# Attention plus GELU MLP on one core: a rewritten front, a moved GEMM fill, and q,k transposes in the score banks

## The chip, the cores and the metric

One core of one Trainium2 chip. The metric is the device time of one execution in microseconds; lower is better. Executions of one kernel on one chip are compared with executions of the kernel before on the same chip. Each ratio below is the mean time of one kernel's fast runs over that of the other's of the same rounds, so not quite the ratio of the medians quoted.

## The reference

Causal attention with a forgetting gate for 8 batches, 8 heads, 576 positions, head size 64, then an MLP with exact GELU over 4608 tokens, 512 to 2048 to 512.

```python
scores = scale * q @ k.T                       # per batch and head
decay  = cum[:, None] - cum[None, :]           # cum = cumsum(log(clip(f)))
attn   = softmax(where(causal, -1e9, scores + decay))
x      = (attn @ v) as [B*S, H*D]
out    = gelu(x @ w_in) @ w_out
```

The decay is folded into v: `wT` holds exp of minus the cumulated log gate, v is multiplied by it, and a 65th column of the AV product gives the softmax's sum.

## The kernel before

For each batch: load q and k (cast to bf16) and v; transpose q and k of four head pairs on TensorE, copy them from PSUM with VectorE; per pair four score tiles, one exp each on ScalarE, causal masks on GpSimd; AV; normalize; transpose into `xT_sb`; then the first GEMM (`gemm1`, 16 blocks of four matmuls, a GELU each). The second GEMM of the batch before (`gemm2`, 64 matmuls) is fed in small pieces ("fill") between the attention steps of the next batch, so that TensorE does not idle behind the exps.

```python
s_psum = tile_pool(name="s_psum", bufs=2, space=PSUM)   # score tiles [P, 2, 512] fp32
o_psum = tile_pool(name="o_psum", bufs=2, space=PSUM)   # AV outputs, transposes
...
    def transposes(b, i, which):
        src = qk_of[b][which]
        ps = o_psum.tile([P, 2, JT // 2, PT], BF16, tag="o", name="ps_t")
        ...                                             # 6 transposes, then 4 copies
    for b in range(B):
        fill = gemm2(b - 1) if b else iter(())
        load_qk(b + 2)
        load_v(b + 2)
        for i in range(HP):
            for t in range(4):
                scores(b, i, t)
                ...                                     # AV of pair i - 1
                take(fill, 2)
        ...
        for ffb in range(n_ff):
            gemm1(b, ffb)
            if b + 1 < B:
                if ffb % 2 == 1:
                    transposes(b + 1, ffb // 4, (ffb // 2) % 2)
```

Each set of transposes, q's or k's, is a tile of its own, and q's and k's of a pair are two gemm1 blocks apart.

The softmax here doesn't subtract the row's maximum and nothing guards it: scores larger than these inputs give would overflow.

Of the kernel before, what the change touches and what calls it, by code (L numbers as in the profile page):

```python
# [8 lines left out]
FP32 = mybir.dt.float32  # L9
# [5 lines left out]
P = 128  # L15
S = 576
# [33 lines left out]
def kernel(  # L50
# [22 lines left out]
    ctx.enter_context(tc.manual_schedule())  # L73

    consts = ctx.enter_context(tc.tile_pool(name="consts", bufs=1))
    qk_pool = ctx.enter_context(tc.tile_pool(name="qk", bufs=2))
    v_pool = ctx.enter_context(tc.tile_pool(name="v", bufs=2))
    e_pool = ctx.enter_context(tc.tile_pool(name="e", bufs=2))
    x_pool = ctx.enter_context(tc.tile_pool(name="x", bufs=3))
    g_pool = ctx.enter_context(tc.tile_pool(name="g", bufs=2))  # L80
    o_pool = ctx.enter_context(tc.tile_pool(name="outs", bufs=4))
# [4 lines left out]

    qk_of, v_of = {}, {}

    def load_qk(b, h0=0, h1=H):
        if b >= B:  # L90
            return
        if b not in qk_of:
            qk_of[b] = (
                qk_pool.tile([PT, H, JT * D], BF16, tag="q", name=f"q{b}"),
                qk_pool.tile([PT, H, JT * D], BF16, tag="k", name=f"k{b}"),
            )
        for src, dst in zip((q, k), qk_of[b]):
            nc.gpsimd.dma_start(  # L98
                dst[:, h0:h1, :],
                src[b, h0:h1].rearrange("h (p j) d -> p h (j d)", j=JT),  # L100
            )

    def load_v(b, h0=0, h1=H):
        if b >= B:
            return
        if b not in v_of:
            v_of[b] = v_pool.tile([P, H, NBLK, D], FP32, tag="v", name=f"v{b}")
        vt = v_of[b]
        for h in range(h0, h1):
            nc.sync.dma_start(  # L110
                vt[:, h, 0:4, :],
                v[b, h, 0:512].rearrange("(n p) d -> p n d", p=P),
            )
        nc.sync.dma_start(
            vt[:, h0:h1, 4, :], v[b, h0:h1, 448:S].rearrange("h p d -> p h d")
        )

    f_sb = consts.tile([BH, S], FP32)
    nc.sync.dma_start(f_sb, f.rearrange("b h s -> (b h) s"))
    for i in range(HP):  # L120
        load_qk(0, 2 * i, 2 * i + 2)
    load_v(0)


    ident_bf = consts.tile([P, P], BF16)
    make_identity(nc, ident_bf)
    ident_fp = consts.tile([P, P], FP32)
    make_identity(nc, ident_fp)
    qA = [consts.tile([P, S], BF16, name=f"qA{i}") for i in range(HP)]
    qB = [consts.tile([P, S], BF16, name=f"qB{i}") for i in range(HP)]  # L130
    kT = [consts.tile([P, S], BF16, name=f"kT{i}") for i in range(HP)]
# [5 lines left out]
    w_out_sb = consts.tile([P, n_ff, d_model], BF16)  # L137
    w_in_r = moe_w_in.rearrange("(ko ki) f -> ki ko f", ki=P)
    w_out_r = moe_w_out.rearrange("(ko ki) dm -> ki ko dm", ki=P)
    for kt in range(n_dm):  # L140
        nc.gpsimd.dma_start(w_in_sb[:, kt, :], w_in_r[:, kt, :])
    load_qk(1)
    load_v(1)
    for kt in range(0, n_ff, 4):
        nc.gpsimd.dma_start(w_out_sb[:, kt : kt + 4, :], w_out_r[:, kt : kt + 4, :])


    wT = consts.tile([P, NBLK, BH], FP32)
# [7 lines left out]
    nc.scalar.activation(lf, f_sb, Act.Ln)  # L156
    nc.vector.tensor_tensor_scan(cum, ones, lf, 0.0, Alu.mult, Alu.add)
    nc.scalar.activation(wk, cum, Act.Exp, bias=cum[:, S // 2 : S // 2 + 1], scale=-1.0)
    psw = o_psum.tile([P, NBLK, BH], FP32, tag="o", name="psw")

    xT_sb = consts.tile([P, n_dm, N_tok], BF16)


    def transposes(b, i, which):

        src = qk_of[b][which]
        ps = o_psum.tile([P, 2, JT // 2, PT], BF16, tag="o", name="ps_t")
        for h in range(2):
            for j in range(JT // 2):
                nc.tensor.transpose(  # L170
                    ps[:, h, j, :],
                    src[:, 2 * i + h, 2 * j * D : 2 * (j + 1) * D],
                    ident_bf[:PT, :PT],
                )
        for h in range(2):
            dst = (qA[i], qB[i])[h] if which == 0 else kT[i]
            rows = dst[h * D : (h + 1) * D, :].rearrange(
                "d (p j two) -> d two p j", j=JT // 2, two=2
            )
            for odd in range(2):  # L180
                nc.vector.tensor_copy(  # L181
                    rows[:, odd],
                    ps[odd * D : (odd + 1) * D, h].rearrange("d j p -> d p j"),
                )

    vw_of = {}

    def weigh_v(b, i):

        if b not in vw_of:  # L190
            vw_of[b] = v_pool.tile([P, H, NBLK, D + 1], BF16, tag="vw", name=f"vw{b}")
        hs = slice(2 * i, 2 * i + 2)
        bh = b * H + 2 * i
        w = wT[:, :, bh : bh + 2].rearrange("p n h -> p h n")
        nc.gpsimd.tensor_tensor(  # L195
            vw_of[b][:, hs, :, 0:D],
            v_of[b][:, hs, :, :],
            w.unsqueeze(3).to_broadcast([P, 2, NBLK, D]),
            Alu.mult,
        )  # L200
        nc.gpsimd.tensor_copy(vw_of[b][:, hs, :, D], w)

    e_of = {}

# [29 lines left out]
    def attend(b, i, h, ms):  # L234
        if (b, i, h) not in o_of:
            o_of[b, i, h] = o_psum.tile([P, NBLK, D + 1], FP32, tag="o", name="o")
        o = o_of[b, i, h]
        for m in ms:
            for n in range(m + 1):
                t, c = where(n, m)  # L240
                nc.tensor.matmul(  # L241
                    o[:, m, :],
                    e_of[b, i, t][:, h, c : c + P],
                    vw_of[b][:, 2 * i + h, n, :],
                    start=(n == 0),
                    stop=(n == m),
                )

    def normalize(b, i, h):
        if (b, i) not in x_of:  # L250
            x_of[b, i] = x_pool.tile([P, NBLK, 2, D], BF16, tag="x", name="x")
        o = o_of[b, i, h]
        r = x_pool.tile([P, NBLK], FP32, tag="r", name="r")
        nc.vector.reciprocal(r, o[:, :, D])  # L254
        nc.vector.tensor_tensor(  # L255
            x_of[b, i][:, :, h, :],
            o[:, :, 0:D],
            r.unsqueeze(2).to_broadcast([P, NBLK, D]),
            Alu.mult,
        )  # L260
# [30 lines left out]
    def gemm2(c):  # L291

        t0 = c * TC
        for ts in range(n_sub):
            ps = m_psum.tile([P, d_model], FP32, tag="m", name="ps2")
            for kt in range(n_ff):
                nc.tensor.matmul(  # L297
                    ps,
                    g_of[c][kt][:, ts * P : (ts + 1) * P],
                    w_out_sb[:, kt, :],  # L300
                    start=(kt == 0),
                    stop=(kt == n_ff - 1),
                )
                if kt == n_ff - 1:
                    ot = o_pool.tile([P, d_model], FP32, tag="ot", name="ot")
                    nc.vector.tensor_copy(ot, ps)  # L306
                    nc.sync.dma_start(
                        out[t0 + ts * P : t0 + (ts + 1) * P, :], ot
                    )
                yield  # L310
# [4 lines left out]
                return  # L315


    for i in range(HP):
        transposes(0, i, 0)
        transposes(0, i, 1)  # L320
    for n in range(NBLK):
        nc.tensor.transpose(psw[:, n, :], wk[:, K0[n] : K0[n] + P], ident_fp[:BH, :BH])
    nc.vector.tensor_copy(wT[:, 0:4, :], psw[:, 0:4, :])
    nc.vector.tensor_copy(wT[D:P, 4, :], psw[D:P, 4, :])
    for i in range(HP):
        weigh_v(0, i)

    for b in range(B):
        fill = gemm2(b - 1) if b else iter(())
        load_qk(b + 2)  # L330
        load_v(b + 2)
        for i in range(HP):
            for t in range(4):
                scores(b, i, t)
                if i:
                    if t == 0:
                        attend(b, i - 1, 0, (4, 3))
                    elif t == 1:
                        attend(b, i - 1, 0, (2, 1, 0))
                        normalize(b, i - 1, 0)  # L340
                    elif t == 2:
                        attend(b, i - 1, 1, (4, 3))
                    else:
                        attend(b, i - 1, 1, (2, 1, 0))
                        normalize(b, i - 1, 1)
                if i >= 2 and t == 1:
                    to_xT(b, i - 2)
                take(fill, 2)
        i = HP - 1
        take(fill, 4)  # L350
        attend(b, i, 0, (4, 3, 2, 1, 0))
        normalize(b, i, 0)
        to_xT(b, i - 1)
        take(fill, 4)
        attend(b, i, 1, (4, 3, 2, 1, 0))
        normalize(b, i, 1)
        take(fill, 8)
        to_xT(b, i)
        take(fill, 999)
        for ffb in range(n_ff):  # L360
            gemm1(b, ffb)
            if b + 1 < B:
                if ffb % 2 == 1:
                    transposes(b + 1, ffb // 4, (ffb // 2) % 2)
                if ffb % 4 == 2:
                    weigh_v(b + 1, ffb // 4)
    take(gemm2(B - 1), 999)
    for c in range(B, n_chunks):
        for ffb in range(n_ff):
# [32 lines left out]
```

## Time and profile before

| | before |
|---|---|
| time, median (4 runs) | 420.5 us (419.2 to 421.5) |
| first gemm1 matmul of batch 0 | 57.84 us |
| first gemm1 matmul of batch 1 | 102.93 us |
| mean period of the batches after it (gemm1 start to gemm1 start) | 42.78 us |
| TensorE busy | 368.4 of 419.1 us |
| ScalarE: table load at 205.06; exps of 1024 and of 384 columns behind it | 1.28; 1.02 and 0.485 us |
| granted clock from 57.84 to 61.46, first eight gemm1 matmuls of batch 0 | 0.50 |

The starts are read from TensorE's timeline. They cut the run into a front, one batch that has to recover from it, six equal batches, and 59 us of closing GEMMs. The lines behind this reading stand in the prediction.

### The profile page before, as it was taken

Reading aid. Unit: us, or ns where it says so; the run is one execution under the profiler, and the core shown is the slowest. Engines: PE = TensorE matmul, PEld = TensorE weight load, DVE = VectorE, ACT = ScalarE, POOL = GpSimd, SP = SyncE. Lnnn points to the kernel's source line nnn. Section 1 sums busy time; section 2 is a strip of 40 time slices with the busy share of each in tenths; the row PEclk is TensorE's granted clock in tenths of the full one; section 3 lists DMA queues with packets and bytes.
Section 4 is the critical chain, followed back from the end, with each engine's and each line's share of the span. In section 5 each row is a group of like instructions: output and inputs, shape, how many; then the busy total and the mean of one; then the engine's idle time right before and its main releaser. Section 6 shows DMA issues by size and latency. Waiting matters only on the chain.

```text
span 419.1 us, 7515 instructions
## 1 busy us (share of the span) xinstructions
PE 368.4 (88%) x3045; PEld 207.5 (50%) x3045; DVE 207.2 (49%) x466; ACT 215.0 (51%) x291; POOL 129.5 (31%) x262
## 2 busy tenths in 40 slices
PE   1340879899989998999899989998999999999996
PEld 1220645465546554655465546654664456444442
DVE  6930339534954486448634773468355924102001
ACT  3040736872677267725773577447743675350620
POOL 8408460446034603460247024700470042000000
PEclk9999969999999999999999999999999999999999
DMA  9999985801671166216521643100001000102002
GB/s 156 209 193 196 193 186 125 114 28 54 148 109 31 51 152 93 48 51 152 82 58 52 152 65 74 46 31 2 27 27 51 2 25 28 50 0 77 25 25 77
DMA packets 62738, 34.19 MB, mean 82 GB/s; under 512 B 43184, under 2 KB 57520, under 8 KB 62704
## 3 DMA queue, kind: packets, MB, share of 16 engines
q0 software_dynamic: 15328, 13.63, 20.9%
q1 hardware_dynamic: 47376, 20.08, 18.7%
q8 instruction: 24, 0.39, 0.4%
q14 instruction: 10, 0.08, 0.1%
HBM read 37.90 MB, written 9.44 MB: 113 GB/s over the span
## 4 chain that ended last, share of the span: by engine, by line
PE 77%; ACT 8%; POOL 5%; issue 4%; DVE 4%; ACTq 0%; POOLq 0%
PE ps L277 30%; PE ps L297 26%; PE s L210 7%; PE o L241 7%; ACT e L220 6%; PE ps_t L170 4%; POOL e L222 3%; PE ps_x L265 2%; DVE kT L181 2%; ACT L220 1%; DVE qB L181 1%; DVE qA L181 1%; POOL vw L195 1%; POOL q L98 1%; POOL k L98 1%
## 5 line engine op out<-in xcount | busy, mean ns | idle before, releaser
L289 ACT ACTIVATE g<-ps 128x512 bf16<-128x512 f32 x144 | 86.0, 597 | 125.7 <-PE ps L277 125.7
L297 PE MATMUL ps<-w_out_sb,g 128*128 128x512 bf16 x576 | 146.2, 379 | 0.0
L277 PE MATMUL ps<-xT_sb,w_in_sb 128*128 128x512 bf16 x576 | 136.5, 383 | 0.0
L220 ACT ACTIVATE e<-s 128x1024 bf16<-128x1024 f32 (+2 forms) x128 | 105.7, 862 | 56.2 <-PE s L210 47.6
L222 POOL TENSOR_SCALAR_AFFINE_SELECT e<-e 128x256 bf16<-128x256 bf16 x160 | 62.5, 406 | 114.7 <-ACT e L220 114.3
L277 PEld LDWEIGHTS <-w_in_sb 128*128 128x128 bf16 x576 | 54.0, 99 | 58.2 <-issue 3.5
L241 PE MATMUL o<-vw,e 128*128 128x65 bf16 x960 | 53.9, 196 | 17.7 <-POOL e L222 9.7
L297 PEld LDWEIGHTS <-g 128*128 128x128 bf16 x576 | 49.4, 98 | 37.8
L254 DVE RECIPROCAL r<-o 128x5 f32<-128x5 f32 x64 | 12.5, 195 | 110.5 <-PE o L241 110.5
L210 PE MATMUL s<-qA,kT 128*128 128x384 bf16 (+2 forms) x192 | 54.6, 289 | 11.3 <-ACT e L220 10.3
L181 DVE COPY kT<-ps_t 64x288 bf16<-64x288 bf16 x128 | 61.3, 479 | 2.5 <-PE ps_t L170 0.3
L306 DVE COPY ot<-ps 128x512 f32<-128x512 f32 x36 | 24.7, 687 | 75.7 <-PE ps L297 75.7
L210 PEld LDWEIGHTS <-kT 128*128 128x128 bf16 x384 | 37.2, 100 | 47.1 <-issue 17.2
L241 PEld LDWEIGHTS <-e 128*128 128x128 bf16 x960 | 45.5, 99 | 29.7 <-POOL e L222 11.3
L210 PE MATMUL s<-qB,kT 128*128 128x384 bf16 (+2 forms) x192 | 49.7, 290 | 0.0
L195 POOL TENSOR_TENSOR vw<-v,wT 128x640 bf16<-128x640 f32 x32 | 40.8, 1276 | 15.9 <-issue 13.1
L181 DVE COPY qA<-ps_t 64x288 bf16<-64x288 bf16 x64 | 30.6, 478 | 13.7 <-PE ps_t L170 12.5
L98 POOL DMA_DIRECT2D q<-in_q_dram x11 | 8.4, 766 | 80.3 <-PE ps_t L170 78.7
L255 DVE TENSOR_TENSOR x<-o,r 128x320 bf16<-128x320 f32 x64 | 31.4, 491 | 2.2
L181 DVE COPY qB<-ps_t 64x288 bf16<-64x288 bf16 x64 | 30.7, 480 | 0.9
L170 PE MATMUL ps_t<-ident_bf,q 96*128 96x96 bf16 x192 | 14.6, 216 | 11.6 <-POOL ident_bf masks.py:199 7.2
L170 PEld LDWEIGHTS <-q 96*128 96x128 bf16 x192 | 12.4, 103 | 18.9 <-issue 7.0
(33 smaller groups left out, 117.2 us busy)
## 6 DMA issues: line engine op xcount, KB each, us to landing
out_dram<-ot SPq DMA_DIRECT2D x36, 256.0 KB, 2.0
v<-in_v_dram SPq DMA_DIRECT2D x64, 128.0 KB, 3.1
q<-in_q_dram POOLq DMA_DIRECT2D x7, 576.0 KB, 6.0
k<-in_k_dram POOLq DMA_DIRECT2D x7, 576.0 KB, 8.0
w_in_sb<-in_moe_w_in_dram POOLq DMA_DIRECT2D x4, 512.0 KB, 12.1
v<-in_v_dram SPq DMA_DIRECT2D x8, 256.0 KB, 3.4
w_out_sb<-in_moe_w_out_dram POOLq DMA_DIRECT2D x4, 512.0 KB, 25.7
q<-in_q_dram POOLq DMA_DIRECT2D x4, 144.0 KB, 6.2
```

The costliest lines, as they stand in the source:

```text
L170: nc.tensor.transpose(ps[:, h, j, :], src[:, 2 * i + h, 2 * j * D : 2 * (j + 1) * D], ident_bf[:PT, :PT],)
L181: nc.vector.tensor_copy(rows[:, odd], ps[odd * D : (odd + 1) * D, h].rearrange("d j p -> d p j"),)
L195: nc.gpsimd.tensor_tensor(vw_of[b][:, hs, :, 0:D], v_of[b][:, hs, :, :], w.unsqueeze(3).to_broadcast([P, 2, NBLK, D]), Alu.mult,)
L210: nc.tensor.matmul(st[:, h, c : c + w], kT[i][:, K0[n] : K0[n] + P], qt[:, q0 : q0 + w], start=True, stop=True,)
L220: nc.scalar.activation(et[:, :, 0:c], st[:, :, 0:c], Act.Exp, scale=scale)
L222: nc.gpsimd.affine_select(out=et[:, :, c0 : c0 + P], in_=et[:, :, c0 : c0 + P], compare_op=Alu.is_ge, fill=0.0, base=0, pattern=[[0, 2], [ ...
L241: nc.tensor.matmul(o[:, m, :], e_of[b, i, t][:, h, c : c + P], vw_of[b][:, 2 * i + h, n, :], start=(n == 0), stop=(n == m),)
L255: nc.vector.tensor_tensor(x_of[b, i][:, :, h, :], o[:, :, 0:D], r.unsqueeze(2).to_broadcast([P, NBLK, D]), Alu.mult,)
L277: nc.tensor.matmul(ps, w_in_sb[:, kt, ffb * P : (ffb + 1) * P], xT_sb[:, kt, t0 : t0 + TC], start=(kt == 0), stop=(kt == n_dm - 1),)
L289: nc.scalar.activation(g_of[c][ffb], ps, Act.Gelu)
L297: nc.tensor.matmul(ps, g_of[c][kt][:, ts * P : (ts + 1) * P], w_out_sb[:, kt, :], start=(kt == 0), stop=(kt == n_ff - 1),)
L306: nc.vector.tensor_copy(ot, ps)
```

## The change

Its intent: bring the first batch's exps and the first GEMM forward by ordering the loads (each gated behind the work that needs the one before), shorten the copies of the first transposes, move the fill to where TensorE waited, and free the AV banks by transposing into the score banks. The diff, cut to its core:

```diff
-    qk_pool = tile_pool(name="qk", bufs=2)      # v likewise
+    qk_pool = tile_pool(name="qk", bufs=1)
-    e_pool = tile_pool(name="e", bufs=2)
+    e_pool = tile_pool(name="e", bufs=3)
...
+    load_qk_tokens(0, 0, 2)
     make_identity(nc, ident_bf) ...
+    load_qk_tokens(0, 2, 4)
+    nc.gpsimd.memset(v_of[0][:, :, 0, 0:1], 0.0)     # gates v's load
+    load_v(0, 0, 4)
+    load_qk_tokens(0, 4, 8)
+    load_v(0, 4, 8)
...
+    def transposes_pe(b, i, in_s=True):
+        if in_s:
+            both = s_psum.tile([P, 2, 512], FP32, tag="s", name="s_t")
+            pss = [both[:, w, :].bitcast(BF16)[:, 0:S].rearrange(...) for w in range(2)]
+        for which in range(2):                        # 0: q, 1: k
+            ps = pss[which] if in_s else o_psum.tile(shape, BF16, tag="o", name="ps_t")
+            ...                                       # 6 transposes into ps
+            ...                                       # 4 VectorE copies out of ps
...
+    def first_attention():                            # exps of batch 0 ahead of AV;
+        ...                                           # w_in, then q,k of batch 1, w_out
+    FILL = [[0, 12, 4, 4], [2, 3, 3, 2], [2, 3, 3, 2], [2, 2, 2, 2], [8, 4, 4, 0]]
+    FILL_1 = [[0, 0, 0, 0], [0, 0, 0, 0], [0, 0, 0, 0], [0, 0, 2, 4], [8, 4, 4, 0]]
...
-                if ffb % 2 == 1:
-                    transposes(b + 1, ffb // 4, (ffb // 2) % 2)
+                at = (8, 12, 15) if b == 0 else (1, 5, 9, 13)
+                if ffb in at:
+                    transposes_pe(b + 1, at.index(ffb))
```

More of the change, by code (lines that the diff above doesn't have):

```diff
@@ L75 @@
     consts = ctx.enter_context(tc.tile_pool(name="consts", bufs=1))
-    qk_pool = ctx.enter_context(tc.tile_pool(name="qk", bufs=2))
-    v_pool = ctx.enter_context(tc.tile_pool(name="v", bufs=2))
-    e_pool = ctx.enter_context(tc.tile_pool(name="e", bufs=2))
+    qk_pool = ctx.enter_context(tc.tile_pool(name="qk", bufs=1))
+    v_pool = ctx.enter_context(tc.tile_pool(name="v", bufs=1))
+    e_pool = ctx.enter_context(tc.tile_pool(name="e", bufs=3))
     x_pool = ctx.enter_context(tc.tile_pool(name="x", bufs=3))
@@ L87, with load_qk_tokens @@
     qk_of, v_of = {}, {}
-    def load_qk(b, h0=0, h1=H):
-        if b >= B:
-            return
+    def load_qk_tokens(b, h0=0, h1=H):
         if b not in qk_of:
-            qk_of[b] = (
-                qk_pool.tile([PT, H, JT * D], BF16, tag="q", name=f"q{b}"),
-                qk_pool.tile([PT, H, JT * D], BF16, tag="k", name=f"k{b}"),
-            )
+            qk_of[b] = [
+                qk_pool.tile([PT, H, JT * D], BF16, tag=n, name=f"{n}{b}")
+                for n in "qk"
+            ]
         for src, dst in zip((q, k), qk_of[b]):
@@ L107, in load_v @@
             v_of[b] = v_pool.tile([P, H, NBLK, D], FP32, tag="v", name=f"v{b}")
-        vt = v_of[b]
-        for h in range(h0, h1):
+        for n in range(NBLK):
             nc.sync.dma_start(
-                vt[:, h, 0:4, :],
-                v[b, h, 0:512].rearrange("(n p) d -> p n d", p=P),
-            )
-        nc.sync.dma_start(
-            vt[:, h0:h1, 4, :], v[b, h0:h1, 448:S].rearrange("h p d -> p h d")
-        )
+                v_of[b][:, h0:h1, n, :],
+                v[b, h0:h1, K0[n] : K0[n] + P].rearrange("h p d -> p h d"),
+            )
     f_sb = consts.tile([BH, S], FP32)
     nc.sync.dma_start(f_sb, f.rearrange("b h s -> (b h) s"))
-    for i in range(HP):
-        load_qk(0, 2 * i, 2 * i + 2)
-    load_v(0)
+    load_qk_tokens(0, 0, 2)
     ident_bf = consts.tile([P, P], BF16)
@@ L128 @@
     make_identity(nc, ident_fp)
+    load_qk_tokens(0, 2, 4)
+    v_of[0] = v_pool.tile([P, H, NBLK, D], FP32, tag="v", name="v0")
+    nc.gpsimd.memset(v_of[0][:, :, 0, 0:1], 0.0)
+    load_v(0, 0, 4)
+    load_qk_tokens(0, 4, 8)
+    load_v(0, 4, 8)
     qA = [consts.tile([P, S], BF16, name=f"qA{i}") for i in range(HP)]
@@ L139, with load_w_in, load_w_out @@
     w_out_r = moe_w_out.rearrange("(ko ki) dm -> ki ko dm", ki=P)
-    for kt in range(n_dm):
-        nc.gpsimd.dma_start(w_in_sb[:, kt, :], w_in_r[:, kt, :])
-    load_qk(1)
-    load_v(1)
-    for kt in range(0, n_ff, 4):
-        nc.gpsimd.dma_start(w_out_sb[:, kt : kt + 4, :], w_out_r[:, kt : kt + 4, :])
+    def load_w_in(c):
+        f4 = slice(c * d_ff // 4, (c + 1) * d_ff // 4)
+        nc.gpsimd.dma_start(w_in_sb[:, :, f4], w_in_r[:, :, f4])
+    def load_w_out():
+        for kt in range(0, n_ff, 4):
+            nc.gpsimd.dma_start(w_out_sb[:, kt : kt + 4, :], w_out_r[:, kt : kt + 4, :])
     wT = consts.tile([P, NBLK, BH], FP32)
@@ L158, with transposes_first @@
     nc.scalar.activation(wk, cum, Act.Exp, bias=cum[:, S // 2 : S // 2 + 1], scale=-1.0)
-    psw = o_psum.tile([P, NBLK, BH], FP32, tag="o", name="psw")
     xT_sb = consts.tile([P, n_dm, N_tok], BF16)
-    def transposes(b, i, which):
-        src = qk_of[b][which]
-        ps = o_psum.tile([P, 2, JT // 2, PT], BF16, tag="o", name="ps_t")
+    def transposes_first(i, which):
+        src = qk_of[0][which]
+        ps = o_psum.tile([P, JT, PT], BF16, tag="o", name="ps_f")
         for h in range(2):
-            for j in range(JT // 2):
+            for j in range(JT):
@@ L170, in transposes, with evac @@
                 nc.tensor.transpose(
-                    ps[:, h, j, :],
-                    src[:, 2 * i + h, 2 * j * D : 2 * (j + 1) * D],
+                    ps[h * D : (h + 1) * D, j, :],
+                    src[:, 2 * i + h, j * D : (j + 1) * D],
                     ident_bf[:PT, :PT],
                 )
-        for h in range(2):
-            dst = (qA[i], qB[i])[h] if which == 0 else kT[i]
-            rows = dst[h * D : (h + 1) * D, :].rearrange(
-                "d (p j two) -> d two p j", j=JT // 2, two=2
-            )
-            for odd in range(2):
-                nc.vector.tensor_copy(
-                    rows[:, odd],
-                    ps[odd * D : (odd + 1) * D, h].rearrange("d j p -> d p j"),
-                )
+        def evac(eng, dst, r0, r1):
+            op = eng.copy if eng is nc.scalar else eng.tensor_copy
+            op(
+                dst[r0:r1, :].rearrange("d (p j) -> d p j", j=JT),
+                ps[r0:r1].rearrange("d j p -> d p j"),
+            )
@@ new lines, in transposes_first @@
+        if which:
+            evac(nc.vector, kT[i], 0, P)
+        else:
+            evac(nc.scalar if i < 2 else nc.vector, qA[i], 0, D)
+            evac(nc.vector, qB[i], D, P)
+    def transposes_pe(b, i, in_s=True):
+        shape = [P, 2, JT // 2, PT]
+        if in_s:
+            both = s_psum.tile([P, 2, 512], FP32, tag="s", name="s_t")
+            pss = [
+                both[:, w, :]
+                .bitcast(BF16)[:, 0:S]
+                .rearrange("p (h j t) -> p h j t", h=2, j=JT // 2)
+                for w in range(2)
+            ]
+        for which in range(2):
+            src = qk_of[b][which]
+            ps = (
+                pss[which]
+                if in_s
+                else o_psum.tile(shape, BF16, tag="o", name="ps_t")
+            )
+            for h in range(2):
+                for j in range(JT // 2):
+                    nc.tensor.transpose(
+                        ps[:, h, j, :],
+                        src[:, 2 * i + h, 2 * j * D : 2 * (j + 1) * D],
+                        ident_bf[:PT, :PT],
+                    )
+            for h in range(2):
+                dst = (qA[i], qB[i])[h] if which == 0 else kT[i]
+                rows = dst[h * D : (h + 1) * D, :].rearrange(
+                    "d (p j two) -> d two p j", j=JT // 2, two=2
+                )
+                for odd in range(2):
+                    nc.vector.tensor_copy(
+                        rows[:, odd],
+                        ps[odd * D : (odd + 1) * D, h].rearrange("d j p -> d p j"),
+                    )
@@ L186, with weigh_v @@
     vw_of = {}
-    def weigh_v(b, i):
+    def weigh_v(b, i, eng=None):
         if b not in vw_of:
@@ L194, in weigh_v @@
         w = wT[:, :, bh : bh + 2].rearrange("p n h -> p h n")
-        nc.gpsimd.tensor_tensor(
+        eng = eng or nc.gpsimd
+        eng.tensor_tensor(
             vw_of[b][:, hs, :, 0:D],
@@ L200, in weigh_v @@
         )
-        nc.gpsimd.tensor_copy(vw_of[b][:, hs, :, D], w)
+        eng.tensor_copy(vw_of[b][:, hs, :, D], w)
     e_of = {}
@@ L315, in take, with attend_pair, load_next, transposes @@
                 return
-    for i in range(HP):
-        transposes(0, i, 0)
-        transposes(0, i, 1)
-    for n in range(NBLK):
-        nc.tensor.transpose(psw[:, n, :], wk[:, K0[n] : K0[n] + P], ident_fp[:BH, :BH])
-    nc.vector.tensor_copy(wT[:, 0:4, :], psw[:, 0:4, :])
-    nc.vector.tensor_copy(wT[D:P, 4, :], psw[D:P, 4, :])
-    for i in range(HP):
-        weigh_v(0, i)
-    for b in range(B):
-        fill = gemm2(b - 1) if b else iter(())
-        load_qk(b + 2)
-        load_v(b + 2)
+    def attend_pair(b, i):
+        for h in range(2):
+            attend(b, i, h, (4, 3, 2, 1, 0))
+            normalize(b, i, h)
+    def first_attention():
+        def load_next():
+            load_qk_tokens(1, 0, 4)
+            load_qk_tokens(1, 4, 8)
+            load_w_out()
+        def transposes(i):
+            transposes_first(i, 1)
+            transposes_first(i, 0)
+        transposes(0)
+        scores(0, 0, 0)
+        scores(0, 0, 1)
+        psw = o_psum.tile([P, NBLK, BH], FP32, tag="o", name="psw")
+        for n in range(NBLK):
+            nc.tensor.transpose(
+                psw[:, n, :], wk[:, K0[n] : K0[n] + P], ident_fp[:BH, :BH]
+            )
+        nc.vector.tensor_copy(wT[:, 0:4, :], psw[:, 0:4, :])
+        nc.vector.tensor_copy(wT[D:P, 4, :], psw[D:P, 4, :])
+        transposes(1)
+        scores(0, 0, 2)
+        scores(0, 0, 3)
+        transposes(2)
+        weigh_v(0, 0, nc.vector)
+        weigh_v(0, 1)
+        for c in range(4):
+            load_w_in(c)
+        for t in range(4):
+            scores(0, 1, t)
+        transposes(3)
+        weigh_v(0, 2, nc.vector)
+        scores(0, 2, 0)
+        scores(0, 2, 1)
+        attend_pair(0, 0)
+        scores(0, 2, 2)
+        scores(0, 2, 3)
+        weigh_v(0, 3)
+        to_xT(0, 0)
+        scores(0, 3, 0)
+        scores(0, 3, 1)
+        attend_pair(0, 1)
+        scores(0, 3, 2)
+        scores(0, 3, 3)
+        load_next()
+        to_xT(0, 1)
+        attend_pair(0, 2)
+        to_xT(0, 2)
+        attend_pair(0, 3)
+        to_xT(0, 3)
+    FILL = [[0, 12, 4, 4], [2, 3, 3, 2], [2, 3, 3, 2], [2, 2, 2, 2], [8, 4, 4, 0]]
+    FILL_1 = [[0, 0, 0, 0], [0, 0, 0, 0], [0, 0, 0, 0], [0, 0, 2, 4], [8, 4, 4, 0]]
+    def attention(b, fill, counts):
         for i in range(HP):
@@ L334 @@
                 scores(b, i, t)
-                if i:
-                    if t == 0:
-                        attend(b, i - 1, 0, (4, 3))
-                    elif t == 1:
-                        attend(b, i - 1, 0, (2, 1, 0))
-                        normalize(b, i - 1, 0)
-                    elif t == 2:
-                        attend(b, i - 1, 1, (4, 3))
-                    else:
-                        attend(b, i - 1, 1, (2, 1, 0))
-                        normalize(b, i - 1, 1)
-                if i >= 2 and t == 1:
-                    to_xT(b, i - 2)
-                take(fill, 2)
+                if i >= 2 and t == 0:
+                    to_xT(b, i - 2)
+                if i and t == 1:
+                    attend(b, i - 1, 0, (4, 3))
+                elif i and t == 2:
+                    attend(b, i - 1, 0, (2, 1, 0))
+                    normalize(b, i - 1, 0)
+                elif i and t == 3:
+                    attend(b, i - 1, 1, (4, 3, 2, 1, 0))
+                    normalize(b, i - 1, 1)
+                if b == 1 and i == 0 and t == 2:
+                    transposes_pe(1, 3, in_s=False)
+                    load_qk_tokens(2)
+                take(fill, counts[i][t])
         i = HP - 1
-        take(fill, 4)
+        take(fill, counts[HP][0])
         attend(b, i, 0, (4, 3, 2, 1, 0))
@@ L353 @@
         to_xT(b, i - 1)
-        take(fill, 4)
+        take(fill, counts[HP][1])
         attend(b, i, 1, (4, 3, 2, 1, 0))
         normalize(b, i, 1)
-        take(fill, 8)
+        take(fill, counts[HP][2])
         to_xT(b, i)
         take(fill, 999)
+    for b in range(B):
+        if b == 0:
+            first_attention()
+            load_v(1)
+        else:
+            load_v(b + 1)
+            attention(b, gemm2(b - 1), FILL_1 if b == 1 else FILL)
         for ffb in range(n_ff):
@@ L362 @@
             if b + 1 < B:
-                if ffb % 2 == 1:
-                    transposes(b + 1, ffb // 4, (ffb // 2) % 2)
+                at = (8, 12, 15) if b == 0 else (1, 5, 9, 13)
+                if ffb in at:
+                    transposes_pe(b + 1, at.index(ffb))
                 if ffb % 4 == 2:
                     weigh_v(b + 1, ffb // 4)
+        if 0 < b < B - 2:
+            load_qk_tokens(b + 2)
     take(gemm2(B - 1), 999)
```

## The prediction

> **What bounds the kernel now.** I read the page's slices first, then the chain of work that ended last, then the timeline of the front and of one steady batch, then the DMA view.
>
> ```profile
> PE   1340879899989998999899989998999999999996
> PEclk9999969999999999999999999999999999999999
> DMA  9999985801671166216521643100001000102002
> ```
> One slice is 10.5 us. TensorE is full from slice 6 on. The first five and a half slices are empty of matmul work and full of transfers. So the kernel has two parts: a front bound by loads and by the order of work, and seven nearly full batches.
>
> ```profile
> 21.78 1.95 DVE L181 COPY kT<-ps_t 64x288 bf16<-64x288 bf16 x4
> 27.91 1.02 ACT L220 ACTIVATE e<-s 128x1024 bf16<-128x1024 f32 x1 [0.72 <-PE s L210]
> 33.39 1.28 POOL L195 TENSOR_TENSOR vw<-v,wT 128x640 bf16<-128x640 f32 x1 [13.08 <-issue]
> 34.89 0.32 PE L241 MATMUL o<-vw,e 128*128 128x65 bf16 x3 [7.01 <-POOL vw L201]
> 40.48 2.55 POOL L222 TENSOR_SCALAR_AFFINE_SELECT e<-e 128x256 bf16<-128x256 bf16 x7
> 43.67 0.92 ACT L220 ACTIVATE e<-s 128x896 bf16<-128x896 f32 x1 [14.73 <-PE s L210]
> 57.84 3.62 PE L277 MATMUL ps<-xT_sb,w_in_sb 128*128 128x512 bf16 x8
> ```
> These timeline lines tell the front. VectorE copies transposes out until 23.7 (32 copies, two to a matrix half), so scores wait. Five exps run, then TensorE, in program order, waits at the first AV for v. GpSimd gets v only at 33.4, because v's load shared the engines with the weights. It then weighs all four pairs, issues two loads and only then masks: exps resume at 43.67. The first GEMM starts at 57.84.
>
> ```profile
> 204.80 0.59 PE L297 MATMUL ps<-w_out_sb,g 128*128 128x512 bf16 x2
> 205.23 0.35 PE L210 MATMUL s<-qA,kT 128*128 128x448 bf16 x1
> 205.42 0.35 PE L210 MATMUL s<-qB,kT 128*128 128x448 bf16 x1
> 205.61 0.59 PE L297 MATMUL ps<-w_out_sb,g 128*128 128x512 bf16 x2
> 207.43 0.30 PE L210 MATMUL s<-qA,kT 128*128 128x320 bf16 x1 [1.23 <-ACT e L220]
> ```
> This is the start of a steady batch. The third score tile waits for the first exp, which waits for a table load at 205.06. Between 204.97 and 210.06 the chain leaves TensorE for ScalarE and GpSimd: 5.1 us, in which TensorE streamed about 3.1 us of work (the rest of one fill 0.26, three fills of two matmuls at 0.43, scores 0.38 + 0.44 + 0.17 + 0.44, three AVs 0.09). So a batch of 42.73 us (gemm1 starts 188.55 to 231.28) has some 2.0 us of stall and 40.7 us of work.
>
> [...] in the window 35 to 42 us:
> ```profile
> q0 software_dynamic: 1102, 1.09, 91.5%
> q1 hardware_dynamic: 1104, 0.27, 29.8%
> ```
> Packets are equal in number, so v (256 B rows) gets 0.27 of 1.36 MB, about 40 GB/s, while weight rows of 1 KB are queued; the total is 196 GB/s. [...] The trace shows 1.28 us, and 1.02 us for 1024 columns, 0.485 for 384. [...] the contiguous 576-column copy of xT takes 0.447 us, the strided 288-column copy 0.479. [...] The eight matmuls at 57.84 took 3.62 us against 1.73 later[...].
>
> **The change part by part.** Loads: pair 0's q,k first, then pair 1's, then half of v, then the rest, with w_in only after GpSimd has weighed pair 1's v. Identities are built after two issues instead of eight: GpSimd reached them at 6.52; now about 1.36 + 0.81 + 0.64 = 2.8. First transposes then depend on the data: about 5.8 instead of 7.24.
>
> First-batch copies: six transposes per head with no parity split, so k is one 576-column copy: [...]0.78 us; q is two, one on ScalarE for the first two pairs (scaling its 0.485 us for 384 columns: 0.645). VectorE has 1.56 us (pairs 0, 1) or 2.34 (2, 3) per pair in place of 3.9. The scan holds VectorE to 7.1, then kT 7.9, qB 8.7 or so, scores 9.0, first exp about 10, against 23.67.
>
> The exps: four per pair, 1.02 + 0.92 + 1.02 + 0.49 = 3.45, in practice 3.67 (46.64 to 50.31). Four pairs are 14.7. I walked the order by hand: exp 2 waits for pair 1's transposes (about 1.5 us idle), to_xT(0) waits in TensorE's order behind the VectorE work for pairs 2 and 3 (about 2), so the last exp ends near 28.5; two more AV pairs with their reciprocals, multiplies and transposes (30 AVs, 0.7 to 1 us of normalize each, 2.5 to 4 us) put the first GEMM at about 32.3. v's first half needs f, q, k and itself, 2.0 MB at about 190 GB/s, from 2.5: landed at 13.5, no wait. **Gain 57.84 - 32.3 = 25.5 us.** gemm1(0) keeps its half-clock start and has three transposes sets instead of four: 18.46 less 0.52 for the missing set[...]: about 17.2 us, ending at 49.5 instead of 76.3.
>
> Batch 1 pays back. Everything up to w_out and the second v must move in any order: f 0.15, two q,k 2.36, two v 2.62, weights 4.2 = 9.3 MB; at 192 GB/s 48.6 us, plus 2.5 start, plus 1 to 2 idle: about 53. load_v(1) starts when v is released at about 25 and gets 40 to 50 GB/s beside w_in, q,k and w_out, so it lands last, near 53 to 54. GpSimd must then weigh four pairs (4 x 1.4 = 5.7) before, in its order, it masks pair 0 (5 x 0.4 = 2.0): 61.7. TensorE reaches the first AV of batch 1 at about 57, so waits 4 to 5. No GEMM fill exists there before the last pair, so what follows runs at ScalarE's pace: the exps left are half a pair and two pairs, 1.02 + 0.49 + 2 x 3.67 = 8.9, from 62 to 71; then TensorE's tail from 70.3: 20 fill matmuls x 0.216 = 4.3, two AV groups and two transposes sets 1.5, together 5.8; then 42 matmuls x 0.216 = 9.1. gemm1(1) starts at about 85.2, against 103.1: **17.9 us of gain survive**.
>
> Steady batches 2 to 7: the 12-matmul fill (2.6 us) after the second scores covers the table load plus first exp (1.28 + 1.03). That removes the 2.0 us stall. But transposes now take a score buffer, and the buffer of pair 3's set is the one the second score tile takes (20 tiles a batch, two buffers). Before, a transposes set waited for the last copy of the tile two back (at 10.01, for qB ended 9.86), so release is of the whole tile. Eight copies x 0.488 = 3.9, started 0.47 after the transposes begin, end 4.4 after; TensorE arrives after transposes 0.52 + two gemm1 blocks 1.73 + scores 0.44 = 2.7. **New stall 1.7.** And no matmuls are left between the last to_xT and gemm1: normalize latency (225.66 to 226.64 = 0.98) against 4 fills of 0.86, then the xT copy behind an output copy of 0.69: 0.1 + 0.37 = about 0.5. Net per batch -2.0 + 1.7 + 0.5 = +0.2, over six batches +1.3. Masks with three e buffers free ScalarE's 0.55 us waits, which are not on the path. The last 59 us do not change.
>
> Sum: 420.5 - 17.9 + 1.3 = 403.9. I move it to 401, since the hand walk of batch 1 stacks several late estimates, and since the second score tile may wait less.
>
> **The rivals.** A: the v(1) landing binds nothing, because it gets a fairer share or because the front's gates leave more room. [...] Against it: the total of 9.3 MB. It would give 4 us: about 397. B: the second score tile does not wait for copies, and the new fill hides the whole steady stall: six times 1.5 to 1.7 more, near 391. Against it: the whole-tile release above. C: the front does not become exp-bound, because VectorE (copies, weighing, normalizing in one queue) or v's second half holds it, and batch 1 runs at half clock with idle gaps as slice 5 of the clock row shows: scores and AVs then take double, 5.2 us a pair against 3.67, 3 to 6 us more: about 408. D: loads are the bound anyhow, so work moves forward but the end of gemm1(1) hardly moves: 412 or more. Against it: before, w_out had landed by about 46 (23 to 27 us after issues from 13 to 20), yet gemm2(0) began only after 76.
>
> **Range and chances.** A and B together reach 388 to 390, C reaches 409, D a little more. Range 389 to 410. Under 412.1 is faster by over 2%: 0.92; within 2%: 0.07; slower: 0.01.
>
> **What would show it.** Right: first exp near 10 us; w_in's first GEMM between 29 and 35; weighing of batch 1 waits on v's DMA until 50 to 55, and TensorE's wait at batch 1's first AV names GpSimd; gemm1(1) starts at 82 to 88; each steady batch's second score tile waits 1.5 to 1.9 us for a kT copy, ScalarE no longer being named at the third; a short gap before gemm1's fourth K step; period 42.5 to 43.2. Wrong: a period near 41 (rival B), a GEMM start after 40, or TensorE waiting for w_in or w_out.

## The result, and the profile after

The changed kernel is slower: 464.1 us median of four runs, 460.0 and 461.3 in the two fast ones, against 420.5; ratio of the fast runs 1.096 (95% interval 1.090 to 1.101). The two other runs (466.9 and 469.5) had a lower granted clock (0.951 and 0.944, against 0.966 and 0.963 in the fast ones) and are not used.

The page's slices for the kernel after (one slice is 11.5 us):

```profile
PE   3878679967998679966998689966998689999996
PEclk9999979979999899998999999998999989999999
```

TensorE works from the start now, but in every batch there is a slice with 6 or 7 tenths where there was 9, and clock slices of 8 beside them. The timeline of the kernel after shows that the front did what was forecast:

```profile
10.00 1.83 ACT L260 ACTIVATE e<-s 128x1024 bf16<-128x1024 f32 x2 [1.57 <-PE s L250]
33.84 7.78 PE L317 MATMUL ps<-xT_sb,w_in_sb 128*128 128x512 bf16 x35
55.30 1.28 POOL L235 TENSOR_TENSOR vw<-v,wT 128x640 bf16<-128x640 f32 x1 [19.56 <-DMA v<-in_v_dram]
```

The first exp comes at 10.0, the first GEMM at 33.84 (57.84 before), and the second batch's v is what GpSimd waits for until 55.3. The loss is in gemm1. These are TensorE's lines (with the wait in brackets), then VectorE's, from one steady batch of the kernel after:

```profile
195.98 0.42 PE L209 MATMUL s_t<-ident_bf,q 96*128 96x96 bf16 x6
198.44 0.41 PE L209 MATMUL s_t<-ident_bf,k 96*128 96x96 bf16 x6 [2.04 <-DVE qB L220]
198.69 3.62 PE L317 MATMUL ps<-xT_sb,w_in_sb 128*128 128x512 bf16 x15
```
```profile
196.43 0.97 DVE L220 COPY qA<-s_t 64x288 bf16<-64x288 bf16 x2 [1.59 <-PE s_t L209]
197.41 0.97 DVE L220 COPY qB<-s_t 64x288 bf16<-64x288 bf16 x2
198.89 1.96 DVE L220 COPY kT<-s_t 64x288 bf16<-64x288 bf16 x4 [0.51 <-PE s_t L209]
```

Six transposes of q, then nothing on TensorE until VectorE's four copies of q have ended at 198.38; six transposes of k start 0.06 us later. K's results go to the other half of the same score tile. The table of waits of the kernel after counts it, and the table of stretches (columns: length, busy time and count per engine, granted clock, DMA share, GB/s) gives gemm1 and the attention part of one steady batch:

```profile
PE s_t L209 <- DVE qB L220: 55.1, 27, 2.0
```
```profile
core 0: us, PE busy (x) PEld busy (x) DVE busy (x) ACT busy (x) POOL busy (x), PEclk, DMA share, GB/s
194.00:220.76 26.76, 18.24 (x114) 9.04 (x114) 15.87 (x34) 8.96 (x15) 6.14 (x10) 0.94 0.38 70
220.76:245.42 24.66, 24.40 (x249) 15.10 (x252) 9.21 (x24) 16.60 (x19) 8.93 (x21) 1.00 0.32 69
```

There are 27 such waits, all sets that went to a score tile. In the kernel before, TensorE's timeline shows no wait between q's and k's transposes of a pair, which stand two gemm1 blocks apart, and the same stretch was 16.0 us long at full clock:

```profile
200.13 0.42 PE L170 MATMUL ps_t<-ident_bf,k 96*128 96x96 bf16 x6
202.11 0.42 PE L170 MATMUL ps_t<-ident_bf,q 96*128 96x96 bf16 x6
204.10 0.42 PE L170 MATMUL ps_t<-ident_bf,k 96*128 96x96 bf16 x6
```
```profile
188.39:204.40 16.01, 16.01 (x114) 8.35 (x113) 13.97 (x29) 9.06 (x16) 0.81 (x1) 1.00 0.42 99
```

Now it takes 26.8 at a mean clock of 0.94, while the attention part behind it became shorter. The lower clock sits after the third wait of the batch: sixteen gemm1 matmuls from 204.85 took 3.62 us at a granted clock of 1.00, the next sixteen (15 recorded), from 211.02, took 5.3 at 0.68 (0.50 between 212 and 214).

The starts of gemm1 in all kernels (e1's only profile fell in a slow execution, so its starts are not given):

| kernel | fast runs, median us | batch 0 | batch 1 | mean period after |
|---|---|---|---|---|
| before | 420.5 | 57.84 | 102.93 | 42.78 |
| after | 460.7 | 33.84 | 89.72 | 51.64 |
| e1 separate AV-bank tiles | 395.3 | | | |
| e2 two score tiles | 404.0 | 33.59 | 83.86 | 42.89 |
| e3 transposes, then copies | 403.4 | 34.45 | 84.36 | 42.86 |
| e5 e1 with even fill | 404.0 | 34.62 | 84.38 | 42.87 |
| e6 before, with the shared tile | 503.2 | 58.39 | 114.42 | 54.70 |
| e7 e1 with w_out later | 392.9 | 33.43 | 83.19 | 41.34 |
| e8 e7 with better fill | 388.7 | 34.37 | 80.01 | 41.27 |

### The profile page after: what moved, and what is told of

It is laid out like the page before. It is cut to its first block, busy times and chain, and to the rows that moved or that the text cites. A ratio compares the mean times of both kernels' runs of the same rounds, so it can differ in the third digit from the quotient of the medians.

```text
span 459.4 us, 7525 instructions
## 1 busy us (share of the span) xinstructions
PE 380.2 (83%) x3044; PEld 211.5 (46%) x3093; DVE 203.3 (44%) x448; ACT 217.0 (47%) x293; POOL 128.7 (28%) x259
## 4 chain that ended last, share of the span: by engine, by line
PE 72%; DVE 12%; DMA 7%; POOL 3%; issue 2%; SPq 1%; ACT 1%; POOLq 0%; DVEq 0%; ACTq 0%
PE ps L337 27%; PE ps L317 25%; PE s L250 9%; PE o L281 6%; DVE qB L220 5%; DVE qA L220 5%; DMA v<-in_v_dram 5%; PE s_t L209 4%; DMA k<-in_k_dram 2%; PE ps_x L305 2%; POOL vw L235 1%; SPq L108 1%; ACT e L260 1%; DVE ot L346 1%; POOL q L97 1%
## 5 line engine op out<-in xcount | busy, mean ns | idle before, releaser
L317 PE MATMUL ps<-xT_sb,w_in_sb 128*128 128x512 bf16 x560 | 141.8, 403 | 2.4 <-issue 1.3
L337 PE MATMUL ps<-w_out_sb,g 128*128 128x512 bf16 x543 | 136.4, 379 | 1.7
L317 PEld LDWEIGHTS <-w_in_sb 128*128 128x128 bf16 x576 | 57.8, 103 | 71.1 <-issue 18.7
L250 PE MATMUL s<-qA,kT 128*128 128x384 bf16 (+2 forms) x192 | 55.2, 297 | 4.8 <-ACT e L260 1.6
L220 DVE COPY kT<-s_t 64x288 bf16<-64x288 bf16 x108 | 51.7, 479 | 15.6 <-PE s_t L209 14.5
L209 PE MATMUL s_t<-ident_bf,k 96*128 96x96 bf16 x162 | 12.0, 214 | 55.1 <-DVE qB L220 55.1
L220 DVE COPY qA<-s_t 64x288 bf16<-64x288 bf16 x54 | 25.7, 476 | 62.4 <-PE s_t L209 62.1
L281 PE MATMUL o<-vw,e 128*128 128x65 bf16 x960 | 44.2, 194 | 1.5 <-POOL e L262 0.8
L281 PEld LDWEIGHTS <-e 128*128 128x128 bf16 x960 | 40.7, 98 | 9.8 <-DVE x L295 1.1
L209 PEld LDWEIGHTS <-k 96*128 96x128 bf16 x168 | 10.8, 102 | 58.0 <-issue 58.0
L220 DVE COPY qB<-s_t 64x288 bf16<-64x288 bf16 x54 | 25.8, 478 | 0.7
```

Of the source, the lines that this page charges most:

```text
L209: nc.tensor.transpose(ps[:, h, j, :], src[:, 2 * i + h, 2 * j * D : 2 * (j + 1) * D], ident_bf[:PT, :PT],)
L220: nc.vector.tensor_copy(rows[:, odd], ps[odd * D : (odd + 1) * D, h].rearrange("d j p -> d p j"),)
L250: nc.tensor.matmul(st[:, h, c : c + w], kT[i][:, K0[n] : K0[n] + P], qt[:, q0 : q0 + w], start=True, stop=True,)
L281: nc.tensor.matmul(o[:, m, :], e_of[b, i, t][:, h, c : c + P], vw_of[b][:, 2 * i + h, n, :], start=(n == 0), stop=(n == m),)
L317: nc.tensor.matmul(ps, w_in_sb[:, kt, ffb * P : (ffb + 1) * P], xT_sb[:, kt, t0 : t0 + TC], start=(kt == 0), stop=(kt == n_dm - 1),)
L337: nc.tensor.matmul(ps, g_of[c][kt][:, ts * P : (ts + 1) * P], w_out_sb[:, kt, :], start=(kt == 0), stop=(kt == n_ff - 1),)
```

## The experiments

All kernels gave the reference's result. Theory T: q's and k's transposes of a pair share one PSUM tile, the program orders the two engines by whole tiles, and so k's transposes wait for q's copies, although the two use different halves of the tile, 2 KB a partition each. Rivals: the new front and loads, the moved fill, the score banks as such, or the reinterpreted bf16 view of an fp32 tile.

**e1: the part undone.** Each set gets its own tile in the AV banks, as before the change.

```diff
-    def transposes_pe(b, i, in_s=True):
+    def transposes_pe(b, i, in_s=False):
```

> Only change: the later batches' q and k transposes go into two separate output tiles again, as before the change; front, fill, loads stay. Theory T (in the changed kernel q and k share one score tile, so k's transposes wait 2.04 us for the four copies of q, 27 times, and the interrupted matmul stream then runs partly at half clock): the wait of the transposes on the qB copies disappears, a steady batch falls from 51.4 to 41.6 us (attention 25.5 + gemm1 16.1), six of them 59 us; batch 1 stays anchored by v's landing at about 55, so the first gemm of batch 1 still starts near 86 to 89. Time about 402. Rival R1 (the new front or the loads cost it): near 460. Rival R2 (the reordered fill costs it, in the attention part): gemm1 parts unchanged at 25.9.

Measured: fast runs 395.1 to 395.5 us against 419.4, ratio 0.941 (0.935 to 0.946). The 65 us between this and the changed kernel all hang on the place of the transposes. The rivals that blame front, loads or fill fall. No wait of transposes on qB is left in the one table of waits of e1, which is of a slow execution, nor in those of e5 and e7, which are built on e1 and were profiled fast. The time is 7 us under the figure expected. No fast profile of e1 shows why, but e5 and e7 start batch 1's gemm1 at 84.4 and 83.2, where I had expected 86 to 89, and e7's period is 41.34, where I had expected 41.6. One of the four executions, the profiled one, took 485.4 us at a mean granted clock of 0.757. It is left out, and its cause is not known.

**e2: two score tiles.** The transposes stay in the score banks; only the sharing goes.

```diff
-            both = s_psum.tile([P, 2, 512], FP32, tag="s", name="s_t")
-            pss = [both[:, w, :].bitcast(BF16)...  for w in range(2)]
+            pss = [s_psum.tile([P, 2, 512], FP32, tag="s", name="s_t")[:, 0, :].bitcast(BF16)...
+                   for w in range(2)]
```

> The transposes stay in the score banks, but q and k get one score tile each. T: the q-to-k wait disappears as in e1, so it is the sharing of a tile and not the choice of banks. Beyond that the prediction's second stall should now show: k's tile of pair 3 is the one that the second score tile of the next batch takes, so that one waits 1.5 to 1.8 us for the last kT copy; period about 43.3, time about 412. If the second score tile does not wait: about 402, as e1. Rival (writing q,k transposes into score banks is itself slow): near 460.

Measured: 404.0 us, ratio 0.962 (0.957 to 0.967). The wait on qB is gone, so it is the sharing and not the banks. What stays against e1 is 8.7 us, and TensorE's timeline and table of waits of e2 name it:

```profile
143.62 0.22 PE L249 MATMUL s<-qB,kT 128*128 128x128 bf16 x1
145.21 0.36 PE L249 MATMUL s<-qA,kT 128*128 128x448 bf16 x1 [1.37 <-DVE kT L219]
145.41 0.35 PE L249 MATMUL s<-qB,kT 128*128 128x448 bf16 x1
```
```profile
PE s L249 <- DVE kT L219: 9.6, 7, 1.4
```

This is the second stall of the prediction: the second score tile takes the buffer of pair 3's k and waits for the last kT copy, 1.4 us seven times. The time is 8 us under the 412 that I expected if the stall showed; the period, 42.89 instead of 43.3, explains 2.5 of them, and batch 1's gemm1, which starts at 83.86 instead of 86 to 89, much of the rest.

**e3: same tile, other order.** All twelve transposes of a pair are issued first, then the eight copies.

```diff
         for which in range(2):
             ...                       # transposes into ps
+            pst.append(ps)
+        for which in range(2):
+            ps = pst[which]
             ...                       # copies out of ps
```

> Same shared score tile as in the changed kernel, only the order of issue differs: all twelve transposes first, then the eight copies. T: with no copy of the tile ahead of k's transposes there is nothing to wait for: gemm1 part 16 us again; second score tile waits 1.5 to 1.9 us as in e2; time about 412. Rival (the shared tile itself, its size or its banks, costs the time whatever the order): near 460.

Measured: 403.4 us, ratio 0.961 (0.955 to 0.967). Tile, banks and work are those of the changed kernel, only the order is another, and 57 us are gone. The score tile's wait for kT is there as in e2 (eight waits, 12.3 us in its table of waits; 1.8 us in each steady batch). Here, too, the time is 8 to 9 us under the 412 expected.

**e4: no reinterpreted view.** The shared tile is declared as bf16.

```diff
-            both = s_psum.tile([P, 2, 512], FP32, tag="s", name="s_t")
+            both = s_psum.tile([P, 2, 1024], BF16, tag="s", name="s_t")
```

> The shared score tile is declared in bf16, so that no reinterpreted view is used. T (waits follow whole tiles): unchanged, 2.04 us waits of k's transposes on the qB copy, time 458 to 470. Rival (the reinterpreted view makes the two halves look alike): waits gone, about 412.

Measured, one run, whose state is therefore unknown: 459.4 us, and the table of waits of e4:

```profile
PE s_t L208 <- DVE qB L219: 55.0, 27, 2.0
```

Nothing changed, so the view is not the cause. In the compiled program, too, the first transpose of k carries a wait on VectorE's semaphore in all 27 sets of the changed kernel and of e4, and in none of e2 and e3. The wait is thus in the program as built: between a copy that reads one half of a tile and a later matmul that writes the other half.

**e6: the harmful part alone.** The kernel before, with q and k of the later batches in one shared score tile.

```diff
-                if ffb % 2 == 1:
-                    transposes(b + 1, ffb // 4, (ffb // 2) % 2)
+                if ffb % 4 == 1:
+                    transposes_pe(b + 1, ffb // 4)      # the changed kernel's, shared tile
```

> The kernel before, with one part of the change alone: q and k transposes of the later batches share one score tile (28 sets), front, loads and fill as before. T: 28 waits x 2.04 = 57 us, and some 1.6 us of half clock in each of seven gemm1 parts, 11 us; part of it may lie beside the stall that the start of a batch has anyway. Time 475 to 490. Rival (the loss needs the new front or the single-buffered loads): 420 to 430.

Measured: 503.2 us, ratio 1.197 (1.191 to 1.203). The one part does the harm without front, fill or single buffers. (It also brings q's and k's transposes together and into the score banks; e2 and e3 do both without this harm.) It is 13 us over the range I gave. The table of waits of e6 shows the 57 us; the table of stretches (columns as above) shows what I had too small:

```profile
PE s_t L206 <- DVE qB L217: 57.0, 28, 2.0
```
```profile
224.25:250.80 26.55, 18.08 (x111) 9.13 (x113) 15.70 (x33) 8.96 (x15) 1.59 (x2) 0.94 0.35 71
169.33:197.54 28.21, 19.58 (x111) 9.57 (x113) 15.96 (x33) 8.96 (x15) 1.58 (x2) 0.88 0.40 79
```

Gemm1 parts of the same kernel take 26.6 or 28.2 us, at 0.94 or 0.88. An estimate: if the clock is either full or half, as in two stretches of the kernel before (the eight matmuls at 57.84 took 3.62 us at a granted clock of 0.50, about twice the 1.89 of the eight at 200.38, at 1.00), 0.88 means 0.24 of 28.2 us at half speed and some 3.4 us lost; 0.94 means 1.6. The loss by the clock varied from batch to batch, and it was mostly the larger one here: five of the six periods of e6 are 54.9 to 55.2 us long, one is 53.3.

**e5: the fill by itself.** e1 with an even fill.

```diff
-    FILL = [[0, 12, 4, 4], [2, 3, 3, 2], [2, 3, 3, 2], [2, 2, 2, 2], [8, 4, 4, 0]]
+    FILL = [[2, 2, 2, 2], [2, 2, 2, 2], [2, 2, 2, 2], [2, 2, 2, 2], [4, 4, 8, 0]]
```

> The kernel of e1 (q and k in two separate output tiles) with the even fill of before: two matmuls of the second GEMM after each score tile, 4 + 4 + 8 and the rest at the end. It measures what the moved fill is worth by itself. As predicted: the stall at the third score tile (first exp behind the table load) comes back, about 2.0 us a batch, the short wait ahead of gemm1 (about 0.5) goes; six batches x 1.5 = 9, so about 404. If the fill is worth nothing: 395, as e1.

Measured: 404.0 us, ratio 0.962 (0.959 to 0.966). The stall of the kernel before is back at the third score tile in the timeline of e5:

```profile
187.80 0.59 PE L337 MATMUL ps<-w_out_sb,g 128*128 128x512 bf16 x2
189.74 0.30 PE L250 MATMUL s<-qA,kT 128*128 128x320 bf16 x1 [1.34 <-ACT e L260]
```

The period is 42.87 against 41.34 in e7, whose steady batches are those of e1: the moved fill is worth 1.5 us a batch, about 9 in all, as predicted.

**e7: w_out after v.** e1 with w_out's load issued behind the first weighing of the second batch's v.

```diff
             load_qk_tokens(1, 4, 8)
-            load_w_out()
...
                     weigh_v(b + 1, ffb // 4)
+                    if b == 0 and ffb == 2:
+                        load_w_out()
```

> The kernel of e1 with w_out's load issued only after the second batch's v has landed (behind the first weighing). In e1's relatives v landed at 49 to 55, and GpSimd weighed and masked late. v should now land at about 41 to 44; the wait of TensorE for the masks of batch 1 (about 1 us) and part of ScalarE's idle time go: 1 to 4 us less than e1, so 391 to 394. If w_out then comes too late for the second GEMM (needed from about 66): TensorE waits for its DMA and nothing is won.

Measured: 392.9 us, ratio 0.936 (0.933 to 0.939). GpSimd's timeline in e7 and the stretches of a steady batch:

```profile
43.35 1.28 POOL L235 TENSOR_TENSOR vw<-v,wT 128x640 bf16<-128x640 f32 x1 [11.01 <-DMA v<-in_v_dram]
```
```profile
207.11:223.90 16.79, 16.44 (x114) 8.46 (x114) 14.47 (x31) 8.96 (x15) 6.14 (x10) 1.00 0.48 96
223.90:248.50 24.60, 24.38 (x250) 15.11 (x252) 10.68 (x27) 16.61 (x19) 8.93 (x21) 1.00 0.41 81
```

V is there at 43.35, and TensorE does not wait for w_out. The 55.3 of the changed kernel is not what this has to be set against: e5, which has e1's loads, had v almost as early, as GpSimd's timeline in e5 shows:

```profile
44.45 1.28 POOL L235 TENSOR_TENSOR vw<-v,wT 128x640 bf16<-128x640 f32 x1 [7.44 <-DMA v<-in_v_dram]
```

So moving w_out brought v forward by about 1 us, and batch 1's gemm1 by 1.2 (84.38 in e5, 83.19 here). The gain over e1, which ran on another chip, is about 2 us, and the intervals of the two ratios overlap, so it is hardly clear of noise. The first of the two stretches, set against 26.76 us in the changed kernel, isolates the price of the shared tile: 9.97 us a batch, of which 4 x 2.04 = 8.16 are waits; the rest, 1.81, fits the lower clock (0.94 against 1.00, some 1.6 us by the estimate made for e6).

**e8: the best version tried.**

```diff
-    FILL = [[0, 12, 4, 4], ..., [8, 4, 4, 0]]
+    FILL = [[0, 10, 4, 4], ..., [6, 4, 5, 0]]
-    FILL_1 = [[0, 0, 0, 0], [0, 0, 0, 0], [0, 0, 0, 0], [0, 0, 2, 4], [8, 4, 4, 0]]
+    FILL_1 = [[0, 0, 0, 0], [0, 0, 4, 4], [4, 4, 4, 4], [4, 4, 4, 4], [7, 4, 5, 0]]
                     transposes_pe(1, 3, in_s=False)
-                    load_qk_tokens(2)
+                if b == 1 and i == 2 and t == 0:
+                    load_qk_tokens(2)
```

> e7 plus fill: batch 1 takes its second-GEMM matmuls from pair 1 on rather than 42 of them at the end (TensorE has slack there while ScalarE is the bound: 32 x 0.216 = 7 us less), every later batch keeps three matmuls for the wait ahead of gemm1 and five for the last normalize (about 0.4 us a batch, six batches), and the third batch's q,k load moves out of the way of the masks. About 383 to 387, faster than both kernels. If w_out has not landed by about 55: TensorE waits for it and the gain shrinks to that of e7.

Measured: 388.7 us (388.3 to 389.2), ratio 0.926 (0.923 to 0.929): faster than both kernels, but short of the 383 to 387 expected. The second batch's gemm1 starts 3.2 us sooner than in e7 and not 7, and the period falls by 0.07 us and not 0.4. What else holds batch 1 was not tried.

## Why the prediction was wrong

The direction was wrong for one reason, and the experiments settle it. The prediction had given "slower" a chance of 0.01.

**The step that failed.** The prediction lets TensorE reach the second score tile after "transposes 0.52 + two gemm1 blocks 1.73 + scores 0.44 = 2.7": it takes the twelve transposes of a pair as one unbroken piece. In the changed kernel they are two pieces with 2.04 us between them. The prediction had the rule in hand, "release is of the whole tile", and used it only for the next owner of a buffer, not for the second half of the same tile. The order in the source (six transposes, four copies, six transposes, one tile) had what was needed. None of the four rivals named it; "TensorE waiting" was looked for at loads and score tiles only.

**What stood in its place.** 27 waits of 2.04 us, 55.1 in all, and part of gemm1 at a lower clock (0.94 in the mean). Between e2 and the changed kernel the spans differ by 459.4 - 401.0 = 58.4 us: 5.9 up to batch 1's gemm1 and 6 x 8.75 = 52.5 in the six periods. A period's 8.75 fits 8.2 of waits plus about 1.7 by the clock (an estimate, between the 1.6 and 1.8 found under e6 and e7) less the 1.4 that the second score tile no longer waits: q's four copies end before k's transposes start, so that only k's four (1.96 us) are left behind them, not eight. That is also why the predicted stall of 1.7 cannot be seen in the changed kernel's steady batches.

**The other steps.** First exp about 10: measured 10.0. VectorE's one-piece copy of k 0.78, the author's estimate: 0.72 to 0.76. First GEMM 32.3: 33.84. Stall of the second score tile 1.7: 1.4. New gap ahead of gemm1 0.5: about 0.3 in e7 (0.1 idle before the last transposes, and the eight first matmuls of gemm1 took 2.14 us, against 1.97 in e8, which keeps three matmuls for it). Net of a steady batch +0.2 us: +0.1, 42.89 in e2 against 42.78. The prediction's own starts of gemm1 before (103.1, 188.55, 231.28) lie about 0.16 us after those of TensorE's timeline, and its 226.64 reads 226.58 there; nothing hangs on that.

The landing of the second v is the other step that does not hold. Predicted at 53 to 54 and to hold up batch 1, it came at 55.3 in the changed kernel. But GpSimd began to weigh that v at 48.96 in e2, 45.49 in e3 and 44.45 in e5, whose loads are written in the same order, and gemm1 of batch 1 began at 83.86, 84.36 and 84.38. So without the overlooked wait an earlier v did not bring that gemm1 forward. This is what rival A supposed, that the landing binds nothing, though the 4 us that A expected from it are not there either. The prediction's 85.2 comes close to these starts by a chain (v lands, is weighed, masks follow) that the three runs do not bear out. What does set them is open; e8's earlier fill moved the start to 80.01.

Sum 403.9 (moved to 401 in the prediction): e2, which is the changed kernel without the overlooked wait, ran 404.0. Much of that agreement is luck, as the start of the first GEMM is 1.5 us late, that of batch 1's gemm1 1.3 early, and the second v 4 to 9 early. Rival B, no wait at the second score tile and so some 391, is what e1 built (395.3).

## What to carry to other kernels

When two things share one on-chip tile, write down the order of issue of all writes and reads of that tile, and ask of each write whether a read stands ahead of it: in this program a tile is what is waited on, not the half of it that is touched. Giving each half its own tile, or issuing all writes before the first read, removed 57 us here (e2, e3); separate tiles in the AV banks removed another 8.7 (e1). When transfers and idle gaps are moved, check the dense stage behind them too: a change of buffers for one stage was paid in another.
